# Group normalisation on one core: half of each sum moved from matmuls to VectorE, squares in two parts about the first element

## The chip, the cores and the metric

The kernel runs on one core of a Trainium2 chip. The metric is device time in microseconds (us) of one execution. Three runs of the kernel before gave 630.66 to 630.94 us, with a median of 630.81. One more execution was profiled; every line of a profile below is from such an execution.

## The reference

A group normalisation of 128 samples with 1024 channels of 32 x 16 elements, in bfloat16. The channels of a sample form 32 groups of 32 channels, so a group has 32 x 512 = 16,384 elements.

```python
G = 32
xr = x.reshape(B, G, C // G, H, W)
mu = xr.mean(axis=(2, 3, 4), keepdims=True)
var = ((xr - mu) ** 2).mean(axis=(2, 3, 4), keepdims=True)
xn = (xr - mu) / jnp.sqrt(var + 1e-5)
return xn.reshape(B, C, H, W) * g[None, :, None, None] + b[None, :, None, None]
```

x has 134 MB and so has the output; g and b have 1024 values each.

## The kernel before

A tile holds four samples: its 128 partitions are 4 samples x 32 groups, and each partition has the F = 16,384 elements of one group (32 KB). There are NT = 32 tiles of 4.19 MB, and six buffers for them, x0 to x5 (SLOTS = 6). A tile is loaded, normalised in place and stored from the same buffer. All synchronisation is written out by hand with semaphores; each engine has its own loop over the tiles.

SyncE (SP) issues the loads (`load`, line 136), one DMA per tile. The load into a buffer waits until the store from that buffer has landed. g and b are loaded after the first tile (lines 147 and 148).

TensorE (`sums`, lines 200 to 206) waits for the load, then sums the tile's 16,384 columns down to 512 with 32 matmuls against an identity matrix, all into one PSUM tile `ps`. The first matmul of a tile (line 203) loads the identity, the other 31 (`again`, line 187) reuse it.

ScalarE (ACT; `squares`, lines 208 to 234) waits for the load. It first takes the negative mean of the tile's first 512 elements of each partition as a shift (line 211, accumulated into `nshift`), then squares the 16,384 elements plus that shift in four parts of 4096 (line 222). Each part's sum goes to a column of `sq`; the squares themselves go to a scratch tile `js` that nothing reads. A part waits for the part before it. After the fourth part has been handed over, ACT issues the store of the tile before (`stored`, that is `late` and `store`, line 140): it waits until that tile is normalised. Then it waits for the variance and takes its square root (line 232).

VectorE (DVE; `normalise`, lines 236 to 297) waits for the matmuls, sums the 512 columns of `ps` into the negative mean (line 239), and waits for the last part of the squares. Three small operations follow, each waiting for the one before: d = negmean - nshift (line 250), nd2 = -d * d (line 254), and the variance from the four sums and nd2 (line 263). After ACT's square root come the reciprocal (line 273), the scale and the bias of each of the 32 channels (lines 275 and 279), and 32 operations of 512 elements that normalise the tile in place (line 289). The last of them releases the store.

GpSimd makes the identity at the start and clears the semaphores at the end. As 32 is no multiple of six, the first round of the loops starts at buffer FIRST = 4; the loops skip the earlier buffers in round one.

Of the kernel before, what the change touches and what calls it, by code (L numbers as in the profile page):

```python
# [1 line left out]

# [5 lines left out]
ACT = mybir.ActivationFunctionType  # L9
ALU = mybir.AluOpType  # L10
F32 = mybir.dt.float32
BF16 = mybir.dt.bfloat16

NUM_GROUPS = 32
EPS = 1e-5

SLOTS = 6
MM_FREE = 512
SQ_PARTS = 4


@with_exitstack
def kernel(
# [13 lines left out]
    nc = tc.nc  # L37
    P = nc.NUM_PARTITIONS
    B0, C, H, W = x.shape
    G = NUM_GROUPS  # L40
    HW = H * W
    KC = C // G
    NS = P // G
    NT = B0 // NS
    F = KC * HW
    inv_n = 1.0 / float(F)
    NMM = F // MM_FREE
    SQ = F // SQ_PARTS

    FIRST = -NT % SLOTS  # L50
    ROUNDS = (NT + FIRST) // SLOTS
# [10 lines left out]
    def sb(name, shape, dtype):  # L62
        return ctx.enter_context(nc.sbuf_tensor(name, shape, dtype))
# [3 lines left out]
    def sem(name):  # L67
        all_sems.append(nc.alloc_semaphore(name))
        return all_sems[-1]

    xs = [sb(f"x{j}", [P, F], BF16) for j in range(SLOTS)]
    ps = [
        ctx.enter_context(nc.psum_tensor(f"ps{j}", [P, MM_FREE], F32))
        for j in range(SLOTS)
    ]

    gam_b = sb("gam_b", [P, KC], BF16)
    bet_b = sb("bet_b", [P, KC], BF16)
    gam = sb("gam", [P, KC], F32)
    bet = sb("bet", [P, KC], F32)  # L80
    eps_t = sb("eps_t", [P, 1], F32)
    warm = sb("warm", [P, 1], F32)
    ones = sb("ones", [P, P], BF16)
    half = sb("half", [P, P], BF16)
    eye = sb("eye", [P, P], BF16)
    ja = sb("ja", [P, HW], BF16)
    js = sb("js", [P, SQ], BF16)
    jd = sb("jd", [P, MM_FREE], BF16)
    jv = sb("jv", [P, SQ_PARTS], F32)

    def small(name, n=1):
        return [sb(f"{name}{j}", [P, n], F32) for j in range(SLOTS)]

    nshift = small("nshift")
    sq = small("sq", SQ_PARTS)
    negmean = small("negmean")
    d = small("d")
    nd2 = small("nd2")
    var = small("var")
    std = small("std")  # L100
    rstd = small("rstd")
    scl = small("scl", KC)
    bia = small("bia", KC)

    def sems(name):
        return [sem(f"{name}{j}") for j in range(SLOTS)]

    s_load = sems("load")
    s_sum = sems("sum")
    s_shift = sems("shift")  # L110
    s_part = [sems(f"part{k}_") for k in range(SQ_PARTS)]
    s_mean = sems("mean")
    s_d = sems("d")
    s_nd2 = sems("nd2")
    s_var = sems("var")
    s_std = sems("std")
    s_rstd = sems("rstd")
    s_scl = sems("scl")
# [11 lines left out]
    sp, pe, act, dve, pool = nc.sync, nc.tensor, nc.scalar, nc.vector, nc.gpsimd  # L130
# [7 lines left out]
    def store(i, j, n):  # L138
        act.wait_ge(s_done[j], n)
        act.dma_start(out=o_v[i], in_=xs[j][:]).then_inc(s_store[j], 16)  # L140
# [10 lines left out]
    for j in range(SLOTS):  # L151
# [7 lines left out]
        out=half[:],  # L159
        in_=ones[:],  # L160
# [8 lines left out]
        out=eye[:],  # L169
        in_=half[:],  # L170
# [11 lines left out]
    dve.wait_ge(s_gbf, 1)  # L182
    pe.wait_ge(s_eye, 1)

    def again(first, rhs, stop):

        return pe.add_instruction(  # L187
            mybir.InstMatmult(
                name=nc.get_next_instruction_name(),
                ins=[pe.lower_ap(rhs), first.ins[1]],  # L190
                outs=[first.outs[0]],
                start_tensor_calc=False,
                stop_tensor_calc=stop,
                tile_size=first.tile_size,
                tile_position=first.tile_position,
                ldweights=False,
            )
        )

    def sums(j, n16):  # L200

        pe.wait_ge(s_load[j], n16)
        m = pe.matmul(out=ps[j][:], lhsT=eye[:], rhs=xs[j][:, 0:MM_FREE], start=True, stop=False)  # L203
        for k in range(1, NMM):
            m = again(m.ins, xs[j][:, k * MM_FREE : (k + 1) * MM_FREE], k == NMM - 1)
        m.then_inc(s_sum[j], 1)

    def squares(j, n16, n, stored):

        act.wait_ge(s_load[j], n16)  # L210
        act.activation(  # L211
            out=ja[:],
            in_=xs[j][:, 0:HW],
            func=ACT.Identity,
            scale=-1.0 / HW,
            accum_out=nshift[j][:],
        ).then_inc(s_shift[j], 1)
        act.wait_ge(s_shift[j], n)
        for k in range(SQ_PARTS):
            if k > 0:  # L220
                act.wait_ge(s_part[k - 1][j], n)
            act.activation(  # L222
                out=js[:],
                in_=xs[j][:, k * SQ : (k + 1) * SQ],
                func=ACT.Square,
                bias=nshift[j][:],
                scale=1.0,
                accum_out=sq[j][:, k : k + 1],
            ).then_inc(s_part[k][j], 1)
        stored()  # L230
        act.wait_ge(s_var[j], n)
        act.activation(  # L232
            out=std[j][:], in_=var[j][:], func=ACT.Sqrt, bias=eps_t[:], scale=1.0
        ).then_inc(s_std[j], 1)

    def normalise(j, n):

        dve.wait_ge(s_sum[j], n)
        dve.tensor_scalar(  # L239
            out=jd[:],  # L240
            in0=ps[j][:],
            scalar1=-inv_n,
            scalar2=None,
            op0=ALU.mult,
            op1=ALU.add,
            accum_out=negmean[j][:],
        ).then_inc(s_mean[j], 1)
        dve.wait_ge(s_mean[j], n)
        dve.wait_ge(s_part[SQ_PARTS - 1][j], n)  # L249
        dve.tensor_tensor(  # L250
            out=d[j][:], in0=negmean[j][:], in1=nshift[j][:], op=ALU.subtract
        ).then_inc(s_d[j], 1)
        dve.wait_ge(s_d[j], n)
        dve.tensor_scalar(  # L254
            out=nd2[j][:],
            in0=d[j][:],
            scalar1=d[j][:],
            scalar2=-1.0,
            op0=ALU.mult,
            op1=ALU.mult,  # L260
        ).then_inc(s_nd2[j], 1)
        dve.wait_ge(s_nd2[j], n)
        dve.tensor_scalar(  # L263
            out=jv[:],
            in0=sq[j][:],
            scalar1=inv_n,
            scalar2=nd2[j][:],
            op0=ALU.mult,
            op1=ALU.add,
            accum_out=var[j][:],  # L270
        ).then_inc(s_var[j], 1)
        dve.wait_ge(s_std[j], n)
        dve.reciprocal(out=rstd[j][:], in_=std[j][:]).then_inc(s_rstd[j], 1)  # L273
        dve.wait_ge(s_rstd[j], n)
        dve.tensor_scalar(  # L275
            out=scl[j][:], in0=gam[:], scalar1=rstd[j][:], scalar2=None, op0=ALU.mult
        ).then_inc(s_scl[j], 1)
        dve.wait_ge(s_scl[j], n)
        dve.scalar_tensor_tensor(  # L279
            out=bia[j][:],  # L280
            in0=scl[j][:],
            scalar=negmean[j][:],
            in1=bet[:],
            op0=ALU.mult,
            op1=ALU.add,
        ).then_inc(s_bia[j], 1)
        dve.wait_ge(s_bia[j], n)
        for k in range(KC):
            v = dve.tensor_scalar(  # L289
                out=xs[j][:, k * HW : (k + 1) * HW],  # L290
                in0=xs[j][:, k * HW : (k + 1) * HW],
                scalar1=scl[j][:, k : k + 1],
                scalar2=bia[j][:, k : k + 1],
                op0=ALU.mult,
                op1=ALU.add,
            )
        v.then_inc(s_done[j], 1)
# [3 lines left out]
    with pe.Fori(16, 16 * ROUNDS + 1, 16) as n16:  # L301
        m16 = pe.snap(n16 - 16)
# [6 lines left out]
    with act.Fori(1, ROUNDS + 1) as n:  # L309
        n16 = act.snap(n * 16)  # L310
        m, m16 = act.snap(n - 1), act.snap(n16 - 16)

        def late(j):

            if j == FIRST:
                with act.If(n > 1):
                    late_store(j - 1, m)
            elif j == 0:
                late_store(SLOTS - 1, m, SLOTS)
            else:  # L320
                late_store(j - 1, n if j > FIRST else m)

        def late_store(j, uses, back=0):
            i = nc.s_assert_within(m * SLOTS + (j - FIRST - back), 0, NT - 1)  # L324
            store(i, j, uses)

        with act.If(n > 1):
            for j in range(FIRST):
                squares(j, m16, m, lambda: late(j))
        for j in range(FIRST, SLOTS):  # L330
            squares(j, n16, n, lambda: late(j))
# [1 line left out]
    act.sem_inc(s_gone, 1)  # L333

    with dve.Fori(1, ROUNDS + 1) as n:
        m = dve.snap(n - 1)
        with dve.If(n > 1):
            for j in range(FIRST):
                normalise(j, m)
        for j in range(FIRST, SLOTS):  # L340
            normalise(j, n)

# [32 lines left out]
```

## Time and profile before

| what | value |
|---|---|
| median of three runs | 630.81 us (630.66 to 630.94) |
| the profiled execution | 630.62 us, of which the span (first to last instruction) is 628.9 us |
| PE (TensorE) busy | 288.5 us |
| DVE busy | 395.0 us |
| ACT busy | 519.5 us |
| moved by DMA | 268.5 MB, on two queues: loads from SP, stores from ACT |
| square of 4096 elements (line 222) | 3708 ns |
| shift pass over 512 elements (line 211) | 624 ns |
| matmul of 512 columns (line 187) | 448 ns mean |
| one normalising operation (line 289) | 412 ns, 32 of them in 10.43 us |

Busy time is the time in which an engine executes instructions; an engine off the path that sets the end may be busy or idle without effect. In the groups of instructions a row gives line, engine, operation, output and inputs, count, and the mean time of one. A window's row gives busy time for each engine (PE, PE's weight load, DVE, ACT, POOL) with the instructions in brackets, then the clock that was granted to TensorE, the DMA share and the GB/s of the packets that start in it. In the timeline a row gives start, duration, engine, line and operation, and in brackets the idle time before it and what ended that. The trace also holds a record of each DMA packet (start, duration, queue and size); a tile is moved in 128 packets of 32 KB, eight for each of the 16 DMA engines, and each engine ends its share with a 4-byte packet that signals the semaphore.

### The profile page before, as it was taken

The numbers are of one execution on the slowest core, as the hardware profiler recorded it, in microseconds if no ns is written. First come the engines' busy times: TensorE is split into PE (matmuls) and PEld (weight loads), VectorE is DVE, ScalarE is ACT, GpSimd is POOL, SyncE is SP. The second block draws the span as 40 slices with busy tenths as digits, with TensorE's granted clock in tenths as the row PEclk, the third lists the DMA queues.
The fourth block names the chain that finished last, engine by engine and source line by source line (L and its number), as shares of the span: only waits on it lengthen the run. The fifth ranks groups of instructions, "written<-read, shape, count | busy, mean of one in ns | idle before, by whom it ended". The sixth has DMA issues, their size and how long they took to land.

```text
span 628.9 us, 3115 instructions
## 1 busy us (share of the span) xinstructions
PE 288.5 (46%) x1024; PEld 3.3 (1%) x32; DVE 395.0 (63%) x1316; ACT 519.5 (83%) x354; POOL 0.8 (0%) x6
## 2 busy tenths in 40 slices
PE   1963565335554335643365533456334654335500
PEld 0000000000000000000000000000000000000000
DVE  0177776666666677765557755577655676556770
ACT  2999999999999999888898888988888988889820
POOL 0000000000000000000000000000000000000000
PEclk9998776667865688666877667876678776778755
DMA  9999999999999999999999999999999999999996
GB/s 366 431 424 415 434 431 431 434 434 434 434 434 431 434 431 434 434 434 434 434 434 434 434 434 431 434 434 434 434 434 434 434 434 434 434 431 434 434 434 281
DMA packets 9484, 268.50 MB, mean 427 GB/s; under 512 B 1288, under 2 KB 1288, under 8 KB 1288
## 3 DMA queue, kind: packets, MB, share of 16 engines
q1 hardware_dynamic: 4872, 134.24, 49.7%
q10 hardware_dynamic: 4608, 134.22, 49.5%
q8 instruction: 1, 0.02, 0.0%
q14 instruction: 3, 0.02, 0.0%
HBM read 134.23 MB, written 134.22 MB: 427 GB/s over the span
## 4 chain that ended last, share of the span: by engine, by line
another core or an unknown queue 43%; ACT 28%; DMA 15%; issue 7%; DVE 3%; ACTq 1%; SPq 1%; DVEq 0%
ACT js L222 26%; DMA out_dram<-x 8%; DMA x<-in_x_dram 7%; DVE x L289 2%; ACT ja L211 1%; ACTq L140 1%; SPq L136 1%; DVE jv L263 0%; DVE nd L254 0%; ACT std L232 0%; DVE d L250 0%; ACTq L324 0%; DVEq L249 0%; DVE bia L279 0%
## 5 line engine op out<-in xcount | busy, mean ns | idle before, releaser
L222 ACT ACTIVATE js<-x,nshift 128x4096 bf16<-128x4096 bf16 x128 | 474.7, 3708 | 4.1
L289 DVE TENSOR_SCALAR x<-x,scl,bia 128x512 bf16<-128x512 bf16 x1024 | 333.7, 412 | 1.2
L187 PE MATMUL ps<-x,eye 128*128 128x512 bf16 x992 | 276.2, 448 | 0.0
L203 PE MATMUL ps<-x,eye 128*128 128x512 bf16 x32 | 18.8, 588 | 305.8 <-DMA x<-in_x_dram 305.8
L250 DVE TENSOR_TENSOR d<-negmean,nshift 128x1 f32<-128x1 f32 x32 | 5.1, 159 | 172.5 <-ACT js L222 172.5
L211 ACT ACTIVATE ja<-x 128x512 bf16<-128x512 bf16 x32 | 20.0, 624 | 51.9 <-DMA x<-in_x_dram 51.4
L239 DVE TENSOR_SCALAR_CACHE_REDUCE jd<-ps 128x512 bf16<-128x512 f32 x32 | 22.2, 693 | 14.7 <-PE ps L187 14.5
L232 ACT ACTIVATE std<-var,eps_t 128x1 f32<-128x1 f32 x32 | 9.4, 294 | 25.8 <-DVE jv L263 25.8
L222 ACT ACTIVATION_READ_ACCUMULATOR js<-x,nshift 128x1 f32 x128 | 23.9, 186 | 0.0
L273 DVE RECIPROCAL rstd<-std 128x1 f32<-128x1 f32 x32 | 5.2, 164 | 11.6 <-ACT std L232 11.6
L279 DVE SCALAR_TENSOR_TENSOR bia<-scl,negmean,bet 128x32 f32<-128x32 f32 x32 | 8.1, 252 | 1.1
L275 DVE TENSOR_SCALAR scl<-gam,rstd 128x32 f32<-128x32 f32 x32 | 7.7, 242 | 1.1
L180 DVE CAST gam<-gam_b 128x32 f32<-128x32 bf16 x1 | 0.2, 181 | 13.0 <-DMA bet_b<-in_b_dram 13.0
L263 DVE TENSOR_SCALAR_CACHE_REDUCE jv<-sq,nd 128x4 f32<-128x4 f32 x32 | 7.0, 217 | 1.1
L254 DVE TENSOR_SCALAR nd<-d 128x1 f32<-128x1 f32 x32 | 6.8, 214 | 1.1
L203 PEld LDWEIGHTS ps<-x,eye 128*128 128x128 bf16 x32 | 3.3, 103 | 582.0 <-DMA x<-in_x_dram 582.0
L211 ACT ACTIVATION_READ_ACCUMULATOR ja<-x 128x1 f32 x32 | 6.0, 186 | 0.0
L239 DVE DVE_READ_ACCUMULATOR jd<-ps 128x1 f32 x32 | 2.8, 89 | 0.0
L263 DVE DVE_READ_ACCUMULATOR jv<-sq,nd 128x1 f32 x32 | 2.7, 83 | 0.0
L178 ACT ACT_TABLE_LOAD x1 | 1.3, 1283 | 1.0 <-ACTq L58 1.0
L155 DVE MEMSET eps_t<- 128x1 f32 x1 | 0.1, 59 | 1.1 <-ACTq L58 1.1
L158 POOL TENSOR_SCALAR_AFFINE_SELECT half<-ones 128x128 bf16<-128x128 bf16 x1 | 0.3, 292 | 0.9 <-DVE ones L156 0.9
(8 smaller groups left out, 1.2 us busy)
## 6 DMA issues: line engine op xcount, KB each, us to landing
x<-in_x_dram SPq DMA_DIRECT2D x32, 4096.0 KB, 32.4
out_dram<-x ACTq DMA_DIRECT2D x32, 4096.0 KB, 49.3
gam_b<-in_g_dram SPq DMA_DIRECT2D x1, 8.0 KB
bet_b<-in_b_dram SPq DMA_DIRECT2D x1, 8.0 KB
```

What stands on the lines that cost most here:

```text
L136: sp.dma_start(out=xs[j][:], in_=x_v[i]).then_inc(s_load[j], 16)
L187: return pe.add_instruction(mybir.InstMatmult(name=nc.get_next_instruction_name(), ins=[pe.lower_ap(rhs), first.ins[1]], outs=[first.outs[0]],
L203: m = pe.matmul(out=ps[j][:], lhsT=eye[:], rhs=xs[j][:, 0:MM_FREE], start=True, stop=False)
L211: act.activation(out=ja[:], in_=xs[j][:, 0:HW], func=ACT.Identity, scale=-1.0 / HW, accum_out=nshift[j][:],).then_inc(s_shift[j], 1)
L222: act.activation(out=js[:], in_=xs[j][:, k * SQ : (k + 1) * SQ], func=ACT.Square, bias=nshift[j][:], scale=1.0, accum_out=sq[j][:, k : k + 1],
L232: act.activation(out=std[j][:], in_=var[j][:], func=ACT.Sqrt, bias=eps_t[:], scale=1.0).then_inc(s_std[j], 1)
L239: dve.tensor_scalar(out=jd[:], in0=ps[j][:], scalar1=-inv_n, scalar2=None, op0=ALU.mult, op1=ALU.add, accum_out=negmean[j][:],).then_inc(s ...
L254: dve.tensor_scalar(out=nd2[j][:], in0=d[j][:], scalar1=d[j][:], scalar2=-1.0, op0=ALU.mult, op1=ALU.mult,).then_inc(s_nd2[j], 1)
L263: dve.tensor_scalar(out=jv[:], in0=sq[j][:], scalar1=inv_n, scalar2=nd2[j][:], op0=ALU.mult, op1=ALU.add, accum_out=var[j][:],).then_inc(s ...
L275: dve.tensor_scalar(out=scl[j][:], in0=gam[:], scalar1=rstd[j][:], scalar2=None, op0=ALU.mult).then_inc(s_scl[j], 1)
L279: dve.scalar_tensor_tensor(out=bia[j][:], in0=scl[j][:], scalar=negmean[j][:], in1=bet[:], op0=ALU.mult, op1=ALU.add,).then_inc(s_bia[j], 1)
L289: v = dve.tensor_scalar(out=xs[j][:, k * HW : (k + 1) * HW], in0=xs[j][:, k * HW : (k + 1) * HW], scalar1=scl[j][:, k : k + 1], scalar2=bi ...
```

## The change

- Sums. TensorE now sums only the first half of each tile: 8192 columns in 16 matmuls. The second half is summed by VectorE, which adds element k of the third quarter to element k of the fourth (4096 pairs) in one operation that also accumulates the total (`sum2`). The pairs' sums go to an 8-bit scratch tile `jp` that nothing reads. The operation stands at the head of `normalise` and waits for the load.
- Identity. It is loaded once, by a matmul of the identity with itself ahead of the loop; all 16 matmuls of every tile reuse it.
- Squares. The shift pass over 512 elements goes. The squares are taken about the first element of each partition (`bias=xs[j][:, 0:1]`, `scale=-1.0`), in two parts of 8192, and written to an 8-bit scratch tile.
- Small operations. sum1 (from `ps`, with the scratch output now in PSUM), the mean from sum1 and sum2, and d (mean against first element, times the root of F) come ahead of the wait for the squares. After the squares: the sum of the two parts, then nvar = d * d - that sum. ACT's square root takes nvar with the scale -1/F.
- Storage. The small per-tile values become columns of one tile for each buffer.

```diff
-SQ_PARTS = 4
+SQ_PARTS = 2
...
-    NMM = F // MM_FREE
-    SQ = F // SQ_PARTS
+    PAIRS = 8 * MM_FREE
+    PE_COLS = F - 2 * PAIRS
+    NMM = PE_COLS // MM_FREE
+    SQ = -(-KC // SQ_PARTS) * HW
+    ROOT = math.isqrt(F)
...
-    js = sb("js", [P, SQ], BF16)
-    jd = sb("jd", [P, MM_FREE], BF16)
+    js = sb("js", [P, SQ], U8)
+    jp = sb("jp", [P, PAIRS], U8)
+    jd = ctx.enter_context(nc.psum_tensor("jd", [P, MM_FREE], F32))
...
+    loaded = pe.matmul(
+        out=ps[0][:, 0:P], lhsT=eye[:], rhs=eye[:], start=True, stop=True
+    ).ins
...
         act.wait_ge(s_load[j], n16)
-        act.activation(
-            out=ja[:],
-            in_=xs[j][:, 0:HW],
-            func=ACT.Identity,
-            scale=-1.0 / HW,
-            accum_out=nshift[j][:],
-        ).then_inc(s_shift[j], 1)
-        act.wait_ge(s_shift[j], n)
         for k in range(SQ_PARTS):
             if k > 0:
                 act.wait_ge(s_part[k - 1][j], n)
+            part = xs[j][:, k * SQ : min((k + 1) * SQ, F)]
             act.activation(
-                out=js[:],
-                in_=xs[j][:, k * SQ : (k + 1) * SQ],
+                out=js[:, 0 : part.shape[1]],
+                in_=part,
                 func=ACT.Square,
-                bias=nshift[j][:],
-                scale=1.0,
+                bias=xs[j][:, 0:1],
+                scale=-1.0,
                 accum_out=sq[j][:, k : k + 1],
             ).then_inc(s_part[k][j], 1)
...
+        dve.wait_ge(s_load[j], n16)
+        dve.scalar_tensor_tensor(
+            out=jp[:],
+            in0=xs[j][:, PE_COLS : PE_COLS + PAIRS],
+            scalar=1.0,
+            in1=xs[j][:, PE_COLS + PAIRS : F],
+            op0=ALU.mult,
+            op1=ALU.add,
+            accum_out=sum2[j][:],
+        )
         dve.wait_ge(s_sum[j], n)
...
+        dve.tensor_scalar(
+            out=negmean[j][:],
+            in0=sum1[j][:],
+            scalar1=sum2[j][:],
+            scalar2=-inv_n,
+            op0=ALU.add,
+            op1=ALU.mult,
         ).then_inc(s_mean[j], 1)
         dve.wait_ge(s_mean[j], n)
+        dve.tensor_scalar(
+            out=d[j][:],
+            in0=xs[j][:, 0:1],
+            scalar1=negmean[j][:],
+            scalar2=float(ROOT),
+            op0=ALU.add,
+            op1=ALU.mult,
+        )
         dve.wait_ge(s_part[SQ_PARTS - 1][j], n)
         dve.tensor_tensor(
-            out=d[j][:], in0=negmean[j][:], in1=nshift[j][:], op=ALU.subtract
-        ).then_inc(s_d[j], 1)
...
+            out=sqsum[j][:], in0=sq[j][:, 0:1], in1=sq[j][:, 1:2], op=ALU.add
+        ).then_inc(s_sqsum[j], 1)
+        dve.wait_ge(s_sqsum[j], n)
+        dve.scalar_tensor_tensor(
+            out=nvar[j][:],
             in0=d[j][:],
-            scalar1=d[j][:],
-            scalar2=-1.0,
+            scalar=d[j][:],
+            in1=sqsum[j][:],
             op0=ALU.mult,
-            op1=ALU.mult,
-        ).then_inc(s_nd2[j], 1)
...
+            op1=ALU.subtract,
+        ).then_inc(s_nvar[j], 1)
```

More of the change, by code (lines that the diff above doesn't have):

```diff
@@ L2 @@
+import math
 from contextlib import ExitStack
@@ L12 @@
 BF16 = mybir.dt.bfloat16
+U8 = mybir.dt.uint8
 NUM_GROUPS = 32
@@ L46 @@
     inv_n = 1.0 / float(F)
-    NMM = F // MM_FREE
-    SQ = F // SQ_PARTS
+    PAIRS = 8 * MM_FREE
[3 more added lines that the diff above has]
+    ROOT = math.isqrt(F)
+    assert ROOT * ROOT == F
     FIRST = -NT % SLOTS
@@ L85, with small @@
     eye = sb("eye", [P, P], BF16)
-    ja = sb("ja", [P, HW], BF16)
-    js = sb("js", [P, SQ], BF16)
-    jd = sb("jd", [P, MM_FREE], BF16)
-    jv = sb("jv", [P, SQ_PARTS], F32)
-    def small(name, n=1):
-        return [sb(f"{name}{j}", [P, n], F32) for j in range(SLOTS)]
[L94 to L101, printed above, removed]
+    js = sb("js", [P, SQ], U8)
+    jp = sb("jp", [P, PAIRS], U8)
+    jd = ctx.enter_context(nc.psum_tensor("jd", [P, MM_FREE], F32))
+    def small(name, n):
+        return [sb(f"{name}{j}", [P, n], F32) for j in range(SLOTS)]
+    scalars = small("scalars", SQ_PARTS + 8)
+    sq = [t[:, 0:SQ_PARTS] for t in scalars]
+    sum1, sum2, sqsum, negmean, d, nvar, std, rstd = (
+        [t[:, k : k + 1] for t in scalars] for k in range(SQ_PARTS, SQ_PARTS + 8)
+    )
     scl = small("scl", KC)
@@ L109 @@
     s_sum = sems("sum")
-    s_shift = sems("shift")
+    s_sums = sems("sums")
     s_part = [sems(f"part{k}_") for k in range(SQ_PARTS)]
     s_mean = sems("mean")
-    s_d = sems("d")
-    s_nd2 = sems("nd2")
-    s_var = sems("var")
+    s_sqsum = sems("sqsum")
+    s_nvar = sems("nvar")
     s_std = sems("std")
@@ L183 @@
     pe.wait_ge(s_eye, 1)
[L185 to L198, printed above, removed]
+    loaded = pe.matmul(
+        out=ps[0][:, 0:P], lhsT=eye[:], rhs=eye[:], start=True, stop=True
+    ).ins
     def sums(j, n16):
         pe.wait_ge(s_load[j], n16)
-        m = pe.matmul(out=ps[j][:], lhsT=eye[:], rhs=xs[j][:, 0:MM_FREE], start=True, stop=False)
-        for k in range(1, NMM):
-            m = again(m.ins, xs[j][:, k * MM_FREE : (k + 1) * MM_FREE], k == NMM - 1)
+        for k in range(NMM):
+            m = pe.add_instruction(
+                mybir.InstMatmult(
+                    name=nc.get_next_instruction_name(),
+                    ins=[
+                        pe.lower_ap(xs[j][:, k * MM_FREE : (k + 1) * MM_FREE]),
+                        loaded.ins[1],
+                    ],
+                    outs=[pe.lower_ap(ps[j][:])],
+                    start_tensor_calc=k == 0,
+                    stop_tensor_calc=k == NMM - 1,
+                    tile_size=loaded.tile_size,
+                    tile_position=loaded.tile_position,
+                    ldweights=False,
+                )
+            )
         m.then_inc(s_sum[j], 1)
@@ L230, in squares, with normalise @@
         stored()
-        act.wait_ge(s_var[j], n)
+        act.wait_ge(s_nvar[j], n)
         act.activation(
-            out=std[j][:], in_=var[j][:], func=ACT.Sqrt, bias=eps_t[:], scale=1.0
-        ).then_inc(s_std[j], 1)
-    def normalise(j, n):
+            out=std[j][:],
+            in_=nvar[j][:],
+            func=ACT.Sqrt,
+            bias=eps_t[:],
+            scale=-inv_n,
+        ).then_inc(s_std[j], 1)
+    def normalise(j, n16, n):
+        dve.wait_ge(s_load[j], n16)
[7 more added lines that the diff above has]
+            accum_out=sum2[j][:],
+        )
         dve.wait_ge(s_sum[j], n)
@@ L241, in normalise @@
             in0=ps[j][:],
-            scalar1=-inv_n,
+            scalar1=1.0,
             scalar2=None,
@@ L245, in normalise @@
             op1=ALU.add,
-            accum_out=negmean[j][:],
+            accum_out=sum1[j][:],
+        ).then_inc(s_sums[j], 1)
+        dve.wait_ge(s_sums[j], n)
+        dve.tensor_scalar(
[5 more added lines that the diff above has]
+            op1=ALU.mult,
         ).then_inc(s_mean[j], 1)
         dve.wait_ge(s_mean[j], n)
+        dve.tensor_scalar(
[5 more added lines that the diff above has]
+            op1=ALU.mult,
+        )
         dve.wait_ge(s_part[SQ_PARTS - 1][j], n)
         dve.tensor_tensor(
-            out=d[j][:], in0=negmean[j][:], in1=nshift[j][:], op=ALU.subtract
-        ).then_inc(s_d[j], 1)
-        dve.wait_ge(s_d[j], n)
-        dve.tensor_scalar(
-            out=nd2[j][:],
+            out=sqsum[j][:], in0=sq[j][:, 0:1], in1=sq[j][:, 1:2], op=ALU.add
[3 more added lines that the diff above has]
+            out=nvar[j][:],
             in0=d[j][:],
-            scalar1=d[j][:],
-            scalar2=-1.0,
+            scalar=d[j][:],
+            in1=sqsum[j][:],
             op0=ALU.mult,
-            op1=ALU.mult,
-        ).then_inc(s_nd2[j], 1)
[L262 to L271, printed above, removed]
+            op1=ALU.subtract,
+        ).then_inc(s_nvar[j], 1)
         dve.wait_ge(s_std[j], n)
@@ L323, in late_store @@
         def late_store(j, uses, back=0):
-            i = nc.s_assert_within(m * SLOTS + (j - FIRST - back), 0, NT - 1)
+            i = nc.s_assert_within(
+                m * SLOTS + (j - FIRST - back),
+                0,
+                NT - 1,
+                skip_runtime_bounds_check_because="m counts from 1 where the rest is negative",
+            )
             store(i, j, uses)
@@ L335 @@
     with dve.Fori(1, ROUNDS + 1) as n:
-        m = dve.snap(n - 1)
+        n16 = dve.snap(n * 16)
+        m, m16 = dve.snap(n - 1), dve.snap(n16 - 16)
         with dve.If(n > 1):
             for j in range(FIRST):
-                normalise(j, m)
+                normalise(j, m16, m)
         for j in range(FIRST, SLOTS):
-            normalise(j, n)
+            normalise(j, n16, n)
     pool.wait_ge(s_gone, 1)
```

## The prediction

> **What bounds the kernel now.** I read the page first, its second and third parts, before any engine's busy time.
>
> ```profile
> span 628.9 us, 3115 instructions
> PE 288.5 (46%) x1024; PEld 3.3 (1%) x32; DVE 395.0 (63%) x1316; ACT 519.5 (83%) x354; POOL 0.8 (0%) x6
> ...
> GB/s 366 431 424 415 434 431 431 434 434 434 434 434 431 434 431 434 434 434 434 434 434 434 434 434 431 434 434 434 434 434 434 434 434 434 434 431 434 434 434 281
> DMA packets 9484, 268.50 MB, mean 427 GB/s; under 512 B 1288, under 2 KB 1288, under 8 KB 1288
> ```
>
> No engine is full, but the transfers are: 434 GB/s in nearly every slice. 268.5 MB at 434 GB/s are 618.7 us of the 628.9; the first slice (366) and the last (281) hold most of the other 10 us. One tile is 4.19 MB in and 4.19 MB out, 19.36 us at 433 GB/s. So work between load and store costs time only where it leaves the transfers without work, which can be at the start, at the end, or if an engine needs over 19.36 us a tile. Next I asked how long transfers queue (the view of line 140):
>
> ```profile
> DMA to landing us min/median/max: 14.1/49.3/53.6
> ```
>
> A store alone takes some 14 us (the last one); the median waits 49 because others are ahead of it. So some 30 us of compute delay per tile would be absorbed in the middle. That leaves the end, read from the timeline of the last tile:
>
> ```profile
> 585.19 0.63 ACT L211 ACTIVATE ja<-x 128x512 bf16<-128x512 bf16 x1 [2.21 <-DMA x<-in_x_dram]
> 597.60 0.34 ACTq L140 DMA_DIRECT2D out_dram<-x  x1
> 601.35 0.16 DVE L250 TENSOR_TENSOR d<-negmean,nshift 128x1 f32<-128x1 f32 x1 [6.33 <-ACT js L222]
> 602.05 0.29 ACT L232 ACTIVATE std<-var,eps_t 128x1 f32<-128x1 f32 x1 [0.81 <-DVE jv L263]
> 603.14 10.43 DVE L289 TENSOR_SCALAR x<-x,scl,bia 128x512 bf16<-128x512 bf16 x32
> 613.60 0.35 ACTq L140 DMA_DIRECT2D out_dram<-x  x1
> ```
>
> The last load lands at 585.16; its store is issued 28.44 us later. Had the transfers been done by then, every us off this chain would count. They were not (windows of the end; the last column is GB/s of the packets that start in the window):
>
> ```profile
> 612.00:613.00 1.00, 0.00 (x0) 0.00 (x0) 1.00 (x4) 0.00 (x0) 0.00 (x0) 0.50 1.21 524
> 613.00:614.00 1.00, 0.00 (x0) 0.00 (x0) 0.56 (x2) 0.00 (x0) 0.00 (x0) 0.50 0.32 131
> 614.00:615.00 1.00, 0.00 (x0) 0.00 (x0) 0.00 (x0) 0.00 (x0) 0.00 (x0) 0.50 1.07 459
> 623.00:624.00 1.00, 0.00 (x0) 0.00 (x0) 0.00 (x0) 0.00 (x0) 0.00 (x0) 0.50 1.06 459
> 624.00:625.00 1.00, 0.00 (x0) 0.00 (x0) 0.00 (x0) 0.00 (x0) 0.00 (x0) 0.50 0.16 66
> 626.00:627.00 1.00, 0.00 (x0) 0.00 (x0) 0.00 (x0) 0.00 (x0) 0.00 (x0) 0.50 0.08 33
> ```
>
> Earlier stores kept the queues full until 613.5; most of the 16 DMA engines then idle some 0.8 us until 614.45. At 459 to 524 GB/s 14 to 16 packets of 32 KB start per us; the 66 in 624:625 are two packets, and one more starts at 626.01 (the packet records; each takes 1.21 us). So 13 DMA engines finish at about 624.3, two at 624.7 and 625.97, and one at 627.22; the program ends 1.7 us after. The records show that the last one finished the store before at 617.54 and then ran its eight packets (8 x 1.21 = 9.7) without a pause. It was never short of work: **the end is that engine's total work, and the last store could have been issued about 3 us later (627.22 - 624.24) for nothing**. That engine falls 0.14 us behind per tile through the whole run (its stores land 19.50 us apart, the others' 19.36).
>
> By the Trainium skill (DMA: Bandwidth & Descriptors, Latency and other measured facts) two of the sixteen are usually slower in traces, with a guess at a cause in descriptor rings that this kernel's queues do not use. The trace agrees that one is slow (627.22 against 624.3), not on why.
>
> **The change, part by part.**
>
> ScalarE. The pass L211 goes (13.88 to 14.63: 0.75 us a tile), and four squares become two. L211's 512 elements take 624 ns and L222's 4096 take 3708: 0.86 ns an element, so 8192 take 3708 + 4096 x 0.86 = 7.23 us, and from one start to the next 0.13 more (3.835 against 3.708). Two are 14.72 against 0.75 + 4 x 3.835 = 16.09. The 8-bit output and the bias read from x itself are in no row. Bounds: 8192 x 0.86 = 7.05 below, 16 of L211's 512 at 624 ns, 9.98, above, at which ScalarE would take over 20 us a tile and be the bound (priced in C); I take 7.23, since two functions gave one rate. Off the chain: 1.37 us.
>
> VectorE's chain after the squares: d, nd and jv (601.35 to 602.05, 0.70) become a sum of two (0.20, d's spacing) and one two-source operation (0.26, jv's spacing): 0.24 less. d and the mean move ahead, under the squares: two operations of 0.25. In all the chain is 1.60 shorter.
>
> VectorE's new pass over 4096 pairs: no row shows it. L239 takes 693 ns for 512 elements and L263's same operation 217 for 4: 0.94 ns an element, 217 + 4092 x 0.94 = 4.05. Bounds: the fast rows of L289, 10.43/32 = 0.326 per 512, give 2.6; the two sources read one after the other, 8192 at 0.94, give 7.9. I take 4.4, near the first, since the two-source L279 (252 ns for 32) stands beside the one-source L275 (242). It lies under the squares: the last tile's VectorE is free from the tile before at 26.84 - 19.36 = 7.5 us after landing, then pass 4.4, the PSUM sum 0.75, mean and d 0.5: 13.2, while the squares end at 14.8. VectorE per tile, one after the other: 4.4 + 13.2 (0.75 + 0.5 + 0.46 + sqrt and three small ones 1.1, normalise 10.4) = 17.6 of 19.36.
>
> Rule and row differ at one point. The Trainium skill (Vector Engine (DVE) Microarchitecture Reference, Points that are easy to get wrong) says that this operation runs at half rate when both sources in SBUF are not bf16. Here both are bf16 and only the output is 8-bit, so by the rule nothing is added; if the output counted too, an estimate by the page is some 8.5 us a pass. No run here shows it yet; a rival below prices the slow pass from rows.
>
> TensorE: 16 matmuls fewer, 16 x 448 ns = 7.2 us a tile; 31 reloads of the identity fewer (0.1 each). Hidden: it is done before the PSUM sum is wanted, also at half clock (9.3 us for 32 in the last tile, so some 5 for 16). One 128-column matmul ahead of the loop lies under the first load.
>
> Stores, the moved wait. Store j is issued by ACT once normalise j is done, but behind the last part of tile j+1's squares. For tile 0, normalise ends at 42.27 and the store goes at 43.36, held by the fourth part at 43.19. After: squares from 13.88 to 28.60, normalise 30.24 to 40.67; the last part of tile 1 has started at 36.7 and no longer holds it, so 40.70, **2.66 earlier**. The store queue does not run empty, as 17.6 us per tile is under 19.36. From then on loads and stores share the DMA engines evenly (loads land 9.7 to 10.7 apart before the first store, 19.36 after), so every us that stores begin earlier puts the last load later by a us: 587.82. Then 587.82 + 26.84 = **614.66 for the last store, 1.06 later than now**, which is the hold that went away (43.36 - 42.27). The cover of 3 us hides it: 13 DMA engines end at 625.3, the late one still at 627.22. If that cover were gone the price is 1.06.
>
> **Sum.** -1.60 on a chain that is not on the path, +1.06 at the last store, hidden: 0. Span 628.9, and 630.62 for that execution; the runs' median is 630.81, 0.19 more. Forecast 630.8, no change; its own range 630.2 to 631.5.
>
> **Rivals.**
>
> A. The shorter chain shows: 628.9 - 1.60 = 627.3, so 629.2. This needs the last load not to move and the late DMA engine not to be late. The slow packets of that engine lie in stretches where compute runs, and its last eight, with every engine silent, were at full pace (9.68 us); fewer instructions might spare it. If it lost nothing, the next ends at 625.97: a gain of 1.25, 629.6. Against: its lag is steady whatever the engines do.
>
> B. The last store decides: 614.66 with all DMA engines waiting for it gives +1.06, 631.9; with a tail chain no shorter than now, +2.66, 633.5. For it: 12 engines already wait 0.8 us. Against: the 3 us of the late one.
>
> C. Slower: the pass over pairs makes VectorE the bound. Its place is each tile's head on VectorE; tile 31 would end at 40.67 + 31 x (13.2 + P). It decides once that passes 616.6, at P = 5.4 us. At P = 7.9: 40.67 + 31 x 21.1 = 694.8, plus the 15.3 us from last issue to end, 710.1, so 712. Squares of 9.98 us would do the same on ScalarE: 2 x 10.1 + 0.9 (its tile period now, 17.04, less 16.1 of work) is 21.1 again. For: nothing in the trace shows a two-source pass of this length. Against: 4.05 by the nearest row.
>
> D. The change does nothing at all to this kernel's order: also 630.8, and it differs from the forecast in the views only (the first store still at 43.4).
>
> **How the numbers follow.** Forecast 0.71, D 0.02, A 0.11, B 0.08 (half of it within 0.2%), C 0.08. 0.2% is 1.26 us, about what a measurement tells from no change. Faster 0.11; same 0.73 + 0.04 = 0.77; slower 0.04 + 0.08 = 0.12. The range takes A's 629.2 and B up to 632.5; C and the rest of B, about 0.1, stay outside.
>
> **What would show it.** ACT's two squares near 7.2 us; the pass over pairs at 4 to 4.5 and VectorE's idle time still ended by ACT; the first store near 40.7; the last load landing near 587.8; the last store near 614.7; 434 GB/s in all middle slices; one or two packets starting alone near 626. Wrong, if middle slices fall under 430, if VectorE is waited for by ACT for several us per tile, or if the last packets end together.

## The result, and the profile after

| | before | changed |
|---|---|---|
| median of six runs | 630.73 us | 650.71 us |
| lowest to highest | 630.51 to 630.94 | 642.67 to 657.96 |
| ratio | | 1.026 (95% interval 1.020 to 1.032) |

The changed kernel is slower, and its time varies from run to run by 15 us where the kernel before repeats within 0.5. The ratio, here and below, leaves out runs over 1.5% above the fastest of the same kernel (here 657.96 and 654.01), so it can lie below the ratio of the medians. The profiled execution of the changed kernel is the longest of the six, 657.96 us; the gap to explain in it is 27 us, in the median 20.

Page of the changed kernel, the lines that answer to those shown before:

```profile
span 656.2 us, 2379 instructions
PE 186.8 (28%) x513; PEld 0.1 (0%) x1; DVE 540.5 (82%) x1380; ACT 472.0 (72%) x162; POOL 0.8 (0%) x6
...
GB/s 374 422 416 437 419 423 427 427 415 427 429 421 411 427 417 431 427 415 431 413 431 425 419 429 419 427 431 421 437 419 443 421 429 439 425 441 348 208 266 264
...
L222 ACT ACTIVATE js<-x 128x8192 uint8<-128x8192 bf16 x64 | 455.7, 7121 | 124.4 <-DMA x<-in_x_dram 122.9
L243 DVE SCALAR_TENSOR_TENSOR jp<-x 128x4096 uint8<-128x4096 bf16 x32 | 141.3, 4415 | 1.1 <-issue 1.1
```

The engines do what was worked out for them: the squares take 7.12 us (forecast 7.23), the pass over pairs 4.415 (4.4). ScalarE waits for loads for 123 us, not for VectorE. What has changed is the line of GB/s: 411 to 443 in the middle where it was 434 in nearly every slice, and 208 to 348 in the last four slices. The transfers themselves have become slower.

The timeline of the first tile shows the step that matters later, first the store's line of the kernel before, then the changed kernel:

```profile
43.36 0.39 ACTq L140 DMA_DIRECT2D out_dram<-x  x1
```

```profile
13.25 7.12 ACT L222 ACTIVATE js<-x 128x8192 uint8<-128x8192 bf16 x1 [10.73 <-DMA x<-in_x_dram]
15.15 4.43 DVE L243 SCALAR_TENSOR_TENSOR jp<-x 128x4096 uint8<-128x4096 bf16 x1 [1.09 <-issue]
27.75 0.16 DVE L281 TENSOR_TENSOR scalars<-scalars 128x1 f32<-128x1 f32 x1 [6.49 <-ACT js L222]
29.28 10.43 DVE L310 TENSOR_SCALAR x<-x,scl,bia 128x512 bf16<-128x512 bf16 x32
39.90 0.39 ACTq L144 DMA_DIRECT2D out_dram<-x  x1
```

The first store goes at 39.90 (43.36 before), as forecast (40.70). And the end, first in windows (last column GB/s), then the last tile's lines of the timeline:

```profile
596.00:616.00 20.00, 5.59 (x16) 0.00 (x0) 17.53 (x46) 14.72 (x5) 0.00 (x0) 0.67 0.78 336
616.00:626.00 10.00, 6.14 (x16) 0.00 (x0) 10.00 (x24) 9.63 (x3) 0.00 (x0) 0.67 0.29 125
636.00:646.00 10.00, 0.00 (x0) 0.00 (x0) 6.79 (x22) 0.00 (x0) 0.00 (x0) 0.50 0.29 125
```

```profile
616.34 7.12 ACT L222 ACTIVATE js<-x 128x8192 uint8<-128x8192 bf16 x1 [4.13 <-DMA x<-in_x_dram]
632.37 10.42 DVE L310 TENSOR_SCALAR x<-x,scl,bia 128x512 bf16<-128x512 bf16 x32
642.82 0.35 ACTq L144 DMA_DIRECT2D out_dram<-x  x1
```

The last load lands at 616.32, 31.16 us later than before (585.16). From there to the last store it takes 26.50 us, 1.94 less than before (28.44). So the chain did get shorter, and the loads cost far more than that. In the packet records about one packet a us starts from 616 to 623 and from 636 to 642: a single DMA engine is at work while the others have nothing left. The rest of the 125 GB/s in 616:626 and 636:646 is the next store, issued at 623.75 and 642.82. Of the last load, the middle one of the 16 engines is done at about 596 and the last at 616; a tile has landed only when its last engine is done. In the kernel before, the last engine was 4.9 us behind the middle one at every load from the fifth on.

The packet records also show when the time goes. A packet of 32 KB takes 1.21 us. Between 60 and 400 us the kernel before has no packet over 1.26; the changed kernel has 417, 289 of them loads, which together take 117 us too long on the 16 engines (87 of them in loads). Sorted by the time since the middle DMA engine closed its share of a store (the "handover" to the next store below):

```
us behind a store's handover   -2.5  -0.5  1.5  3.5  5.5  7.5  9.5  11.5  13.5  15.5
time lost in 2 us, us          22.6  41.3  24.2 4.0  3.0  4.5  3.9  2.5   6.0   5.1
```

Three quarters of it (88 of 117) lie within 6 us around the handover of one store to the next, not evenly over the tile. It is the loads' loss that gathers there; the stores' 30 us are spread over the tile. And up to about 360 us the stores' handovers come some 2.5 to 3.3 us behind those of the loads; in the kernel before they come 9.5 us behind, in every tile until the loads end.

### The profile page after: what moved, and what is told of

It is laid out like the page before. It is cut to its first block, busy times and chain, and to the rows that moved or that the text cites. A ratio compares the mean times of both kernels' runs of the same rounds, so it can differ in the third digit from the quotient of the medians.

```text
span 656.2 us, 2379 instructions
## 1 busy us (share of the span) xinstructions
PE 186.8 (28%) x513; PEld 0.1 (0%) x1; DVE 540.5 (82%) x1380; ACT 472.0 (72%) x162; POOL 0.8 (0%) x6
## 4 chain that ended last, share of the span: by engine, by line
another core or an unknown queue 55%; DVE 20%; DMA 15%; issue 4%; ACT 3%; SPq 1%; ACTq 0%; DVEq 0%
DVE x L310 13%; DMA x<-in_x_dram 8%; DMA out_dram<-x 7%; DVE jp L243 5%; ACT js L222 3%; SPq L140 1%; DVE jd L253 1%; ACT scalars L232 0%; DVE bia L300 0%; DVE scalars L285 0%; DVE scl L296 0%; DVE scalars L263 0%; DVE scalars L272 0%; DVE scalars L294 0%
## 5 line engine op out<-in xcount | busy, mean ns | idle before, releaser
L222 ACT ACTIVATE js<-x 128x8192 uint8<-128x8192 bf16 x64 | 455.7, 7121 | 124.4 <-DMA x<-in_x_dram 122.9
L198 PE MATMUL ps<-x,eye 128*128 128x512 bf16 x512 | 186.5, 544 | 433.6 <-DMA x<-in_x_dram 433.6
L243 DVE SCALAR_TENSOR_TENSOR jp<-x 128x4096 uint8<-128x4096 bf16 x32 | 141.3, 4415 | 1.1 <-issue 1.1
L232 ACT ACTIVATE scalars<-scalars,eps_t 128x1 f32<-128x1 f32 x32 | 9.4, 294 | 34.1 <-DVE scalars L285 34.1
L253 DVE TENSOR_SCALAR_CACHE_REDUCE jd<-ps 128x512 f32<-128x512 f32 x32 | 22.1, 691 | 0.0
L222 ACT ACTIVATION_READ_ACCUMULATOR js<-x 128x1 f32 x64 | 11.9, 186 | 0.0
L300 DVE SCALAR_TENSOR_TENSOR bia<-scl,scalars,bet 128x32 f32<-128x32 f32 x32 | 8.0, 251 | 1.1
L296 DVE TENSOR_SCALAR scl<-gam,scalars 128x32 f32<-128x32 f32 x32 | 7.7, 241 | 1.1
L272 DVE TENSOR_SCALAR scalars<-x,scalars 128x1 f32<-128x1 bf16 x32 | 6.8, 214 | 1.6 <-DVE scalars L263 0.5
L285 DVE SCALAR_TENSOR_TENSOR scalars<-scalars 128x1 f32<-128x1 f32 x32 | 7.0, 219 | 1.1
```

What stands on the lines that cost most here:

```text
L198: m = pe.add_instruction(mybir.InstMatmult(name=nc.get_next_instruction_name(), ins=[pe.lower_ap(xs[j][:, k * MM_FREE : (k + 1) * MM_FREE] ...
L222: act.activation(out=js[:, 0 : part.shape[1]], in_=part, func=ACT.Square, bias=xs[j][:, 0:1], scale=-1.0, accum_out=sq[j][:, k : k + 1],). ...
L232: act.activation(out=std[j][:], in_=nvar[j][:], func=ACT.Sqrt, bias=eps_t[:], scale=-inv_n,).then_inc(s_std[j], 1)
L243: dve.scalar_tensor_tensor(out=jp[:], in0=xs[j][:, PE_COLS : PE_COLS + PAIRS], scalar=1.0, in1=xs[j][:, PE_COLS + PAIRS : F], op0=ALU.mult ...
L253: dve.tensor_scalar(out=jd[:], in0=ps[j][:], scalar1=1.0, scalar2=None, op0=ALU.mult, op1=ALU.add, accum_out=sum1[j][:],).then_inc(s_sums[ ...
L272: dve.tensor_scalar(out=d[j][:], in0=xs[j][:, 0:1], scalar1=negmean[j][:], scalar2=float(ROOT), op0=ALU.add, op1=ALU.mult,)
```

## The experiments

Three theories stood after this. **Pass**: VectorE's pass over pairs, reading beside ScalarE and TensorE, slows the transfers. **Output**: the 8-bit scratch writes do. **Phase**: the moment at which the first store joins the loads sets how the two streams lie against each other for the rest of the run. The first four runs told these apart.

**The kernel before with 8-bit squares** (e4).

```diff
-    js = sb("js", [P, SQ], BF16)
+    js = sb("js", [P, SQ], mybir.dt.uint8)
```

> The kernel before, with one thing changed: the squares' scratch output is 8-bit instead of bfloat16. Pass theory (VectorE's pass over pairs slows the transfers that run beside it): 630.5 to 631.2, middle slices at 434 GB/s. Output theory (8-bit writes into SBUF slow them): 642 to 658, slices at 410 to 430. Phase theory (the earlier first store sets the transfers of the 16 DMA engines against each other): 630.5 to 631.2, as the first store stays at 43.4.

Measured 630.79 (630.46 to 631.13), ratio 1.000 (0.9991 to 1.001). The output theory falls, as far as the squares go.

**The kernel before with 8-bit squares and the pass over pairs** (e6).

```diff
+        dve.wait_ge(s_load[j], n16)
+        dve.scalar_tensor_tensor(
+            out=jp[:],
+            in0=xs[j][:, F // 2 : 3 * F // 4],
+            scalar=1.0,
+            in1=xs[j][:, 3 * F // 4 : F],
+            op0=ALU.mult,
+            op1=ALU.add,
+            accum_out=jacc[j][:],
+        )
         dve.wait_ge(s_sum[j], n)
```

> The kernel before with 8-bit squares (for the room) and the pass over pairs added at the head of VectorE's work on a tile, its sum not used; TensorE keeps 32 matmuls, ScalarE its shift pass and four squares. Pass theory: 642 to 660. Output theory: as the kernel before with 8-bit squares alone. Phase theory: near 631, since the first store is not before 43.4.

Measured 630.80 (630.72 to 631.16), ratio 1.0001 (0.9991 to 1.0011). The pass, 8-bit output included, costs nothing.

**The changed kernel without the pass** (e5).

```diff
-    PE_COLS = F - 2 * PAIRS
+    PE_COLS = F
...
-        dve.scalar_tensor_tensor(
-            out=jp[:],
...
-            scalar1=sum2[j][:],
+            scalar1=0.0,
```

> The changed kernel without the pass over pairs: TensorE sums all 16,384 columns in 32 matmuls again, with the identity still loaded once, two squares to 8 bits, and the first store early. Pass theory: 630 to 631.5 and 434 GB/s. Output theory: 642 to 658. Phase theory: 642 to 658, as the first store goes at about 39.9.

Measured 653.14 (643.41 to 653.95, four runs), ratio 1.028 (1.019 to 1.036): as slow as the changed kernel, though what the change is named for is gone. The first store goes at 40.08.

**The changed kernel with half the pass** (e7).

```diff
-    PAIRS = 8 * MM_FREE
+    PAIRS = 4 * MM_FREE
```

> The changed kernel with the pass cut to half: 2048 pairs on VectorE, 12,288 columns in 24 matmuls. Pass theory: half the loss, 636 to 646. Output and phase theories: unchanged at 642 to 658.

Measured 652.88 (644.78 to 654.33), ratio 1.036 (1.034 to 1.037); first store at 40.17. No half loss. The profiled execution is the shortest of its five, 644.78, and it too has slow packets (280 over 1.26 us between 60 and 400 us, 240 of them loads) and 425 GB/s in 100:200. Of the three, phase is left, and beside it anything else that the changed kernel does in every tile (a "steady" theory). The next four moved the first store. In p2 and p1 no later tile is changed. p4 and p5 also issue every later store after the third part of the squares, but both in the same way: between these two only five operations of tile 0 differ.

**The changed kernel with its first store later** (p2 with two multiplications, p1 with one). In the first round VectorE copies the PSUM sum once more and multiplies parts of tile 0 by one, ahead of the last operation of tile 0 (the edit of p2):

```diff
+        if j == FIRST:
+            with dve.If(n < 2):
+                dve.tensor_scalar(
+                    out=dl[:], in0=ps[j][:], scalar1=1.0, scalar2=None, op0=ALU.mult
+                ).then_inc(s_dl, 1)
+                dve.wait_ge(s_dl, 1)
+                for k in range(2):
+                    dve.tensor_scalar(
+                        out=xs[j][:, k * 4096 : (k + 1) * 4096 - 512 * (k == 3)],
+                        in0=xs[j][:, k * 4096 : (k + 1) * 4096 - 512 * (k == 3)],
+                        scalar1=1.0,
+                        scalar2=None,
+                        op0=ALU.mult,
+                    )
...
```

> The changed kernel with one addition: in the first round alone VectorE repeats some work before the last normalising operation of tile 0 (a copy of the PSUM sum and two multiplications by one in place), so that the first store goes some 3 us later, near 43; all else, and every later tile, as changed. Phase theory (when the first store joins the loads decides how the two streams lie against each other on the DMA engines for the whole run): back to 630 to 632, middle slices at 434. Steady theory (something that the changed kernel does in every tile, such as squares of 8192 or a bias read from x, slows the transfers): 642 to 658 still.

> The same with one multiplication instead of two, so that the first store goes near 41.8, half way. Phase theory: anything from 630 to 658, and with it where the change-over lies. Steady theory: 642 to 658.

p2: first store at 42.94, 631.08 (630.40 to 637.08), ratio 1.001 (0.999 to 1.003). p1: 41.95, 630.78 (629.40 to 648.61), ratio 1.0005 (0.998 to 1.003). Two to three microseconds of idle repetition, once in the run, give back twenty. Not in every run: p1 has one of 648.61, so the change-over lies near. The profiled execution of p2 is one of its two slower runs, 635.58: its middle DMA engine closes the last load at 581.53, near the 580.30 of the kernel before, but its last engine is 11.2 us behind that one (4.9 before).

**The kernel before with its first store earlier** (p4 leaves out 8 operations of tile 0 in the first round, p5 three).

```diff
             ).then_inc(s_part[k][j], 1)
-        stored()
+            if k == SQ_PARTS - 2:
+                stored()
...
-        for k in range(KC):
-            v = dve.tensor_scalar(
+        def norm(k):
+            return dve.tensor_scalar(
...
+        norm(0)
+        if j == FIRST:
+            with dve.If(n > 1):
+                for k in range(1, 9):
+                    norm(k)
+        for k in range(9 if j == FIRST else 1, KC):
+            v = norm(k)
```

> The kernel before with its first store early: ACT issues a store after the third part of the squares, not the fourth, and 8 of the 32 normalising operations of tile 0 are left out in the first round (their part of the output stays as loaded), so that the first store goes near 39.8. Phase theory: 642 to 658, slices at 410 to 430, though no operation of the change is in it. Steady theory: 630.5 to 631.5.

> The same with 3 of tile 0's operations left out in the first round, first store near 41.4. Phase theory: anything from 630 to 658, the same side as the changed kernel with the short delay. Steady theory: 630.5 to 631.5.

p4: first store at 39.77, 652.30 (649.90 to 654.70), ratio 1.035 (1.032 to 1.038). The kernel before, with none of the change's operations, is as slow as the changed one once its first store goes as early. p5: 41.44, 633.01 (630.74 to 636.10), ratio 1.004 (1.002 to 1.007). As p5 shares the moved issue of the later stores, that move alone does not cost the 20 us. The steady theory falls. Windows of p4, then of p2:

```profile
100.00:200.00 100.00, 43.76 (x154) 0.52 (x5) 72.10 (x238) 87.63 (x60) 0.00 (x0) 0.71 1.00 421
300.00:400.00 100.00, 49.20 (x165) 0.52 (x5) 64.88 (x216) 84.27 (x58) 0.00 (x0) 0.70 1.00 434
```

```profile
100.00:200.00 100.00, 28.22 (x80) 0.00 (x0) 96.59 (x255) 85.50 (x29) 0.00 (x0) 0.64 1.00 434
```

The old kernel's operations run at 421 GB/s, the changed kernel's at 434: the rate goes with the first store. In 300:400 p4 is back at 434; its handovers have by then moved from 2.4 to 14 us behind the loads'.

What about the phase is bad? It could be either earliness as such, or the distance of the handovers. The next four went on to both sides.

**Earlier still** (p7: the changed kernel with 8 operations left out, in the manner of p4; p8: 22 left out, and the store of tile 0 issued behind the first square of tile 1, a place that the loop gives to one store in six) **and later still** (p6 and p3: the delay of p2 with three and four multiplications).

```diff
-        stored()
+            if k == (0 if j == FIRST + 1 else SQ_PARTS - 1):
+                stored()
```

> The changed kernel with its first store still earlier: 22 of the 32 normalising operations of tile 0 are left out in the first round (their part of the output stays as loaded) and the store of tile 0 is issued after the first of the two squares of tile 1; it goes near 32.5. Handover theory (transfers slow down only where a store and a load hand over to the next one within some 4 us of each other): the first store's packets start near the middle of load 3, so the handovers of stores and loads lie some 10 us apart; 434 GB/s in the middle and few slow packets. The last load lands some 11 us later than in the kernel before, and the last store then decides the end: 635 to 638. Earliness theory (the earlier the first store, the worse): over 650.

> The changed kernel with 8 of tile 0's normalising operations left out in the first round, first store near 37.3: its first packets fall on the start of load 4, so that stores and loads hand over nearly together. Handover theory: 640 to 660, with slow packets around each handover. Earliness theory: worse than the changed kernel, over 650.

> The changed kernel with the first store delayed by one multiplication more than in the long delay, to about 44.2. Handover theory: handovers some 10 us apart, 629.5 to 631.5, no slow packets, and steadier than the long delay. Steady theory: 642 to 658.

> The same with two multiplications more, first store near 45.3. Handover theory: handovers some 12 us apart, 629.5 to 631.5.

p8: first store at 33.00, 635.00 (634.85 to 635.46), ratio 1.007, where the handover theory had it (635 to 638). p7: 37.51, 631.75 (631.38 to 632.12), ratio 1.0016 (1.0006 to 1.0026). p6: 44.24, 629.80 (629.45 to 636.15), ratio 1.000 (0.998 to 1.001). p3: 45.16, 629.77 (629.57 to 631.75), ratio 0.999 (0.998 to 0.9999).

Earliness falls with p7 and p8, which store earlier than the changed kernel and do not share its loss. My handover theory was half wrong: p7, expected at 640 to 660, has handovers 1.6 us apart, stores ahead of loads, and not one packet over 1.26 between 60 and 400 us. So in these runs it is not nearness on either side that goes with the loss, but stores handing over 2 to 4 us behind the loads. The distance was read off each run and not set by itself. And p6, expected steady and without slow packets, has four of ten runs at 631.6 to 636.2; the profiled one, 636.15, has 81 slow load packets between 60 and 400 us with its handovers 10 to 11 us apart.

p7 and p8 also settle the forecast's account of the end. Their first packets of a store start 5.8 and 9.7 us earlier than in the kernel before (41.26 and 37.38 against 47.07), the last load lands 6.3 and 9.0 later (591.45 and 594.15), the last store goes 4.4 and 7.5 later (617.96 and 621.08), and the spans are 1.4 and 4.5 longer (630.3 and 633.4): each the last store's delay less 3.0, the cover that the prediction read from the late DMA engine.

**Loads and stores alone** (c1 to c4). Whether the engines' work on the tiles has any part in it: sums, squares and normalising are gone, and VectorE only holds tile 0 back by a number of multiplications by one.

```diff
+        dve.wait_ge(s_load[j], n16)
+        if j == FIRST:
+            dve.tensor_copy(out=d[j][:], in_=eps_t[:])
+            with dve.If(n < 2):
+                for k in range(HOLD):
+                    v = dve.tensor_scalar(
+                        out=xs[j][:, k % KC * HW : (k % KC + 1) * HW],
+                        in0=xs[j][:, k % KC * HW : (k % KC + 1) * HW],
+                        scalar1=1.0,
+                        scalar2=None,
+                        op0=ALU.mult,
+                    )
...
+        dve.tensor_copy(out=d2[j][:], in_=eps_t[:]).then_inc(s_done[j], 1)
```

> Loads and stores alone: no sums, no squares, no normalising; the output is x. VectorE multiplies parts of tile 0 by one in the first round, 79 times, only to let the first store go where the changed kernel has it, near 40. Every other tile may be stored as soon as it has landed. Transfer theory (the two streams of transfers do it by themselves): slow packets around each handover, slices at 410 to 430, 636 or more. Compute theory (it needs the engines' reads and writes of SBUF): 434 GB/s, 620 to 630.

> The same with 90 multiplications, first store near 43.4 as in the kernel before. Both theories: 434 GB/s, 620 to 630; by the transfer theory at least 8 below the same with the store near 40.

Both missed their mark: a multiplication by a constant took 0.21 us here (16.31 us for 79), not the 0.33 of a normalising operation, and the first stores went at 31.55 and 33.60. That puts the handovers 4.8 and 9.5 us apart, and the times are 630.51 (630.07 to 631.46) and 628.00 (627.90 to 628.49). Neither run tells the theories apart. The next two aimed again.

> Loads and stores alone again, with 70 multiplications: first store near 29.9, its first packets some 2.5 us behind the start of load 3, as they are behind that of load 4 in the changed kernel, and the stores' handovers some 3 us behind the loads'. Transfer theory: slow packets at each handover, 636 or more. Compute theory: 434 GB/s, 627 to 631.

> The same with 67 multiplications, first store near 29.3 and handovers some 2 us apart. Transfer theory: 636 or more. Compute theory: 627 to 631.

c3: first store at 29.76, handovers 2.3 to 2.9 us apart, 634.71 (633.63 to 649.14), ratio 1.005 (1.004 to 1.007) against the kernel before; the profiled execution is the one of 649.14, the other four lie at 633.63 to 634.83, just under the 636 that the transfer theory had named. c4: 28.96, handovers 19.2 us apart (that is 0.2 ahead, a tile being 19.4), 628.18 (627.77 to 630.29), where I had expected some 2 us behind and the loss. Windows of c3, then of c4 (VectorE, ScalarE and GpSimd busy, clock, DMA share, GB/s):

```profile
60.00:100.00 40.00, 0.31 (x2) 0.00 (x0) 0.00 (x0) 1.00 1.00 414
100.00:200.00 100.00, 0.92 (x6) 0.00 (x0) 0.00 (x0) 1.00 1.00 423
```

```profile
60.00:100.00 40.00, 0.31 (x2) 0.00 (x0) 0.00 (x0) 1.00 1.00 433
100.00:200.00 100.00, 0.92 (x6) 0.00 (x0) 0.00 (x0) 1.00 1.00 433
```

All engines are silent (0.92 us of VectorE in 100), and the 16 DMA engines are never without work (share 1.00). Still c3 moves 414 and 423 GB/s where c4 moves 433, with 0.8 us between their first stores. Every run of c3 is over every run of c4 (633.63 and up against 630.29 and down), 6.5 us apart in the medians. So the transfers can lose time by themselves. That they alone lose as much as the 20 us of the changed kernel is shown by one run of c3 in five; what the engines' work adds is not shown. Nor is the loss made up alike: in the profiled c3 most of it (93 of 132 us between 60 and 400 us) lies in stores, spread over the tile, and the loads' 39 us near the handovers; in p4 too the stores lose more than the loads.

All runs in one table, sorted by the distance; the times are medians:

| run | first store at, us | stores' handover behind the loads', us | time, us (lowest to highest) |
|---|---|---|---|
| p4, before, early | 39.77 | 2.1 to 2.4 | 652.30 (649.90 to 654.70) |
| c3, transfers alone | 29.76 | 2.3 to 2.9 | 634.71 (633.63 to 649.14) |
| changed kernel | 39.90 | 2.5 to 3.3 | 650.71 (642.67 to 657.96) |
| e7, half the pass | 40.17 | 2.3 to 3.8 | 652.88 (644.78 to 654.33) |
| e5, no pass | 40.08 | 3.5 to 4.0 | 653.14 (643.41 to 653.95) |
| c1, transfers alone | 31.55 | 4.8 | 630.51 (630.07 to 631.46) |
| p5, before, less early | 41.44 | 5.0 | 633.01 (630.74 to 636.10) |
| p1, short delay | 41.95 | 7.1 | 630.78 (629.40 to 648.61) |
| p2, long delay | 42.94 | 7.5 to 8.6 | 631.08 (630.40 to 637.08) |
| e6, before with the pass | 43.06 | 9.0 to 9.3 | 630.80 (630.72 to 631.16) |
| kernel before | 43.36 | 9.5 | 630.73 (630.51 to 630.94) |
| c2, transfers alone | 33.60 | 9.5 | 628.00 (627.90 to 628.49) |
| e4, before, 8-bit squares | 43.29 | 9.6 | 630.79 (630.46 to 631.13) |
| p6, delay of three | 44.24 | 9.8 to 11.5 | 629.80 (629.45 to 636.15) |
| p8, earliest | 33.00 | 12.1 | 635.00 (634.85 to 635.46) |
| p3, delay of four | 45.16 | 12.1 to 12.4 | 629.77 (629.57 to 631.75) |
| p7, earlier | 37.51 | 17.4 to 17.8 | 631.75 (631.38 to 632.12) |
| c4, transfers alone | 28.96 | 19.2 | 628.18 (627.77 to 630.29) |

The distance is read from one profiled execution of each, at every third tile; in the slow kernels from the tiles before the spread of the DMA engines moved it. Every kernel with 2 to 4 us loses, whatever it computes. Between 5 and 12 us some runs of some kernels lose (p5, p1, p2, p6), most do not. The distance in p1's run of 648.61 is not known, as it is not the profiled one. The changed kernel itself does not fit all the way: its handovers leave the 2 to 4 us at about 360 us, and still it moves 424 and 428 GB/s in 300:400 and 400:500. p8's loss is the end, told above.

## Why the prediction was wrong

Right, by its own steps:
- The squares (7.12 us against 7.23), the pass over pairs (4.415 against 4.4, and hidden: e6 adds it at 0.01%), the shorter chain at the end (1.94 against 1.60).
- The first store ahead of its old time (39.90 against 40.70; 0.6 of the 0.8 between them is an earlier landing of the first load), and that some 3 us of delay of the last store are covered: p7 and p8 confirm the cover to 0.1 us of span. They also bear out that earlier stores move the last load back by about as much (6.3 for 5.8, 9.0 for 9.7), where the transfers keep their rate.
- Rival C did not come: the pass took 4.415 us, near the 4.05 of the nearest row.

Wrong is the step **"Stores, the moved wait"**, where it says that from the first store on "loads and stores share the DMA engines evenly" and prices the earlier store at 1.06 us, hidden. It took the 434 GB/s of the trace as given wherever the queues are full. The rate depends on the order of the two streams: with the handovers 9.5 us apart the two streams run at 434, with 2 to 4 us they run at 421 to 428 in windows of 100 us. In the profiled execution the term came out as 31.16 us on the last load, 3.1 of it from the earlier first packet (47.07 to 43.99; the forecast had 2.66), and 28.1 from slower transfers that the sum does not contain. Read another way, 15.5 of the 31.16 fall on all the engines (the middle one is done with the last load at 595.83 against 580.30) and 15.6 on the last engine alone, which is 20.5 us behind the middle one in place of 4.9. At the end: 31.16 - 1.94 = 29.2 on the last store, and the span grew by 27.3; the 1.9 between them is what the cover came to here, worked out backwards. The prediction had named its own sign of being wrong, middle slices under 430, and that is what came.

None of the rivals had it. B had the right place (the last store decides, because the last load is later) with a price of 1 to 2.7 us.

What stays open is why a store's handover 2 to 4 us behind a load's is slow and one 0.2 to 1.6 ahead is not, and 5 and more behind only in some runs. The runs show that a loss comes without any engine's work, that in the changed kernel most of it lies in load packets next to the handovers (in c3 and p4 more in store packets), and that in the changed kernel one DMA engine falls behind more than the others (20 us by load 20), so that each landing waits for it. They do not show what the DMA engine waits for in a slow packet, whether the late engine keeps the loss going once the handovers have moved, nor why the loss differs from run to run of one kernel (642.67 to 657.96).

## What to carry to other kernels

A kernel that is bound by transfers can lose several per cent to a change that touches none of them, if it moves the moment at which one stream joins the other; before blaming the new operations, put them alone into the old kernel, and move that moment alone in both. A time that varied by per cents where it used to repeat was the hint here. With its first store held back by 5 us (p3) the changed kernel takes 629.77 us, at most 0.2% ahead of the kernel before (ratio 0.998 to 0.9999). Loads and stores alone take 628.00 in the same six buffers (c2), so there is little left to win in the computation.

## What the runs showed of the hardware

- Two full streams on the same 16 DMA engines ran at 432 to 435 GB/s or at 414 to 426 GB/s (windows from 60 to 500 us of the profiled executions, 628.18 and 649.14) with nothing but 0.8 us between the starts of the stores (c4 and c3).
- Slow packets took up to 2.6 us in place of 1.21. Over the changed kernel's profile the loads lost 129 us and the stores 42; in c3 the stores lost more than the loads (93 us against 39 between 60 and 400 us).
- Around the first packet of the very first store loads were slow in every kernel: 23 to 31 load packets took over 1.26 us within 4 us of it. In the kernel before these are 28 packets that start between 44 and 50 us and took 1.3 to 2.1 us.
- A pass of VectorE over two bfloat16 sources with an 8-bit output and an accumulated sum took 4415 ns for 4096 pairs, 1.08 ns a pair; a square of 8192 elements with 8-bit output 7121 ns.
